# Head of an inducing-point attention and maxout kernel: GpSimd takes the second half of w2−w1, half of w1 comes a second time as fp16, and the first half of hwd is one VectorE copy with two factors

## The chip, the cores and the metric

The kernel runs on one core of one Trainium2 chip. The metric is the device time of one execution in microseconds. Three runs of the kernel before gave 324.2 (median), 323.96 and 324.99.

## What is computed

The reference, cut to what matters (x is 4 × 12544 × 128, inducing 32 × 128, w1 and w2 128 × 1024, w_out 1024 × 128, all fp32):

```python
def mab(q, kv):
    s = scale * (q @ kv.transpose(0, 2, 1))
    s = s - s.max(-1, keepdims=True)
    a = np.exp(s)
    a /= a.sum(-1, keepdims=True) + 1e-09
    return a @ kv
h = mab(I, x)                 # 32 inducing points read the batch
attn = mab(x, h)              # every token reads the 32 results
h1, h2 = attn @ w1, attn @ w2
out = np.maximum(h1, h2) @ w_out
```

The kernel uses max(h1, h2) = h1 + relu(h2 − h1). A token's attention row is a weighted mean of 32 rows of h, so h·(w2−w1), a 32 × 1024 matrix called `hwd`, is made once for each batch, and so is h·(w1·w_out), called `m1`. A token then needs its 32 exponentials e, relu(e·hwd)·w_out + e·m1, and a division by the sum of e.

## The kernel before, in words

**Stages.** The head handles batch 0 alone. It loads x as fp16 (the load casts) in eleven parts, transposes them on TensorE (steps `T`, line 235), copies them from PSUM to SBUF on VectorE or ScalarE (`C`, 246 and 249), scores them against the inducing points (`S`, 258), exponentiates (`X`, 274), and sums h (`H`, 303) and the weights (`E`, 286). After that come the small steps that make `hT`, `hwd` and `m1` of batch 0. The main loop then streams all 392 chunks of 128 tokens of the four batches, and prepares the next batch beside them. All instructions of an engine run in the order in which they are written, so a waiting instruction holds up everything behind it on that engine.

**The head's order** is written out by hand in the string `HEAD` (lines 744 to 750). A letter picks a function, the numbers are its arguments. The last two lines of it, from `h` on, and the two `A` steps and `N0.0` in the lines above, are what this study is about:

- `L` i is `load_x(1, i)` (line 166), a DMA of a part of batch 1, issued by GpSimd. Before all of them GpSimd has issued the loads of batch 0, the four loads of `wf` (line 214: w1 and w2 in fp32, in halves: w1 low, w2 low, w1 high, w2 high) and `woutp` (line 215).
- `A0.2` and `A1.2` are `cast_w1` (774): GpSimd casts the low and the high half of w1 from `wf` to the fp16 tile `w1h`.
- `N0.0` and `N1.0` are `difference` (779): VectorE makes the low and the high half of `w21` = w2 − w1.
- `h` is `small_hT` (451, VectorE), `e` is `small_es` (464, ScalarE), `s` is `small_sums` (490 on TensorE, then 494 and 495 on VectorE): it gives `rs`, the reciprocal of the weight sum, and `rw`, that times 1/scale.
- `D` is `small_hwd0`: a matmul hT × w21 (476) and a copy from PSUM to `hwd` times `rw`, on VectorE (479) or ScalarE (482). `D0.1` makes columns 0 to 255 on ScalarE, `D1.0` columns 256 to 511 on VectorE, `D2.1` columns 512 to 1023 on ScalarE.
- `G0` and `G1` are `score` of blocks 0 and 1 (610, TensorE), `Y` their exponentials (629, ScalarE): `Y0.1` columns 0 to 255 of block 0, `Y0.2` columns 256 to 511, `Y1` all of block 1.
- `W0.1` and `W1.0` are `weights_2`: four transposes of a half of `w1h` (546), copied to `w1T` on ScalarE (552) or VectorE (549). `w` is `weights_3`: w1T × woutp (559), copied to `w1out` on ScalarE (567), from which `small_m1` (518, 526) is made.
- `P0` and `P1` are the first two phases of the main loop.

**A phase** (`phase`, line 1069) is one round of matmuls for four units, one in each quarter of TensorE's rows. Each unit fills a PSUM bank with 512 columns of e·hwd; a relu then empties it on ScalarE (1085) or VectorE (1088). `P0` reads `hwd` columns 0 to 511 and e columns 0 to 255. `P1` reads columns 512 to 1023 of `hwd` in its first quarter. The products relu × woutp (876) follow, an output tile is divided by the sum of e (671 to 681, 907) and stored. Matmuls on a constant tile (833) fill places in which the planner expects TensorE to wait.

**Banks and planner.** Eight PSUM banks serve everything. A model clock in the program (`ck`) decides at build time which bank is taken (the one that the model has free first), which engine gets a relu, and what comes next in the main loop. At the first phase and after the head the model's times are overwritten with fixed numbers; the banks get the times by their rank, so the numbers of the banks may change places while the sequence of the jobs stays.

Of the kernel before, what the change touches and what calls it, by code (L numbers as in the profile page):

```python
# [12 lines left out]
ALU = mybir.AluOpType  # L13
# [89 lines left out]
def kernel(  # L103
# [9 lines left out]
    nc = tc.nc  # L113
    B, N, C = x.shape
    M = inducing.shape[0]
    J = moe_w1.shape[1]
# [3 lines left out]
    scale = 1.0 / math.sqrt(C)  # L120
    P1 = 14
# [17 lines left out]
    ck = Clock()  # L139
    uid = [0]  # L140

    def bank(shape, dtype=F32, only=None):
        i = min(range(8), key=lambda j: ck.bank[j]) if only is None else only
        uid[0] += 1
        return i, psum.tile(shape, dtype, name=f"ps{uid[0]}", tag=f"bank{i}", bufs=1)
# [14 lines left out]
    def load_x(b, i, after=None):  # L160
        k0, n = parts[b][i]
        if after is not None:

            nc.gpsimd.tensor_copy(out=pace, in_=after)  # L164
        for lo, hi in ((0, 65), (65, 128)) if b == 0 and i in (4, 5) else ((0, 128),):
            nc.gpsimd.dma_start(out=xn_at[b, i][lo:hi, 0:n, :], in_=xr[b, lo:hi, k0 : k0 + n, :])  # L166
# [18 lines left out]
    w1h = relup.tile([128, 4096], F16, name="w1h", tag="relu1")[:, 0:J]  # L185
    w21 = consts.tile([C, J], F16, name="w21")
    woutp = consts.tile([128, NJB, C], F16, name="woutp")
    w1T = consts.tile([128, NJB, C], F16, name="w1T")
    w1out = consts.tile([C, C], F16, name="w1out")
# [7 lines left out]
    with tc.manual_schedule(engines={ET.PE, ET.DVE, ET.Activation, ET.Pool, ET.SP}):  # L197
# [14 lines left out]
        for lo in (0, 512):  # L212
            for w, src in enumerate((moe_w1, moe_w2)):
                nc.gpsimd.dma_start(out=wf[:, w, lo : lo + 512], in_=src[:, lo : lo + 512])
        nc.gpsimd.dma_start(out=woutp, in_=moe_w_out.rearrange("(jb j) c -> j jb c", j=128))
        nc.vector.memset(warm, 0.0)
        nc.vector.memset(ones16, 1.0)
# [6 lines left out]
        st = [dict() for _ in range(B)]  # L224
# [242 lines left out]
        def small_hwd0(n, eng=0):  # L467
            if "hwd" not in st[0]:
                st[0]["hwd"] = smp.tile([128, J], F16, name="hwd_0", tag="hwd")
            hwd = st[0]["hwd"]  # L470
            lo, w = ((0, 256), (256, 256), (512, 512), (512, 256), (768, 256))[n]
            bi, ps = bank([128, 512])
            ps = ps[:, 0:w]
            sl = slice(lo, lo + w)
            ck.wait(max(ck.bank[bi], st[0]["hT4r"]), "p1")
            nc.tensor.matmul(out=ps, lhsT=st[0]["hT4"], rhs=w21[:, sl], start=True, stop=True)
            end = ck.run(0.215 * w / 512)
            if eng == 0:
                nc.vector.tensor_scalar(out=hwd[:, sl], in0=ps, scalar1=st[0]["rw"], scalar2=None, op0=ALU.mult)
                ck.bank[bi] = ck.on_dve(end, 0.07 + w / 970.0)  # L480
            else:
                nc.scalar.activation(out=hwd[:, sl], in_=ps, func=AF.Copy, scale=st[0]["rw"])  # L482
                ck.bank[bi] = ck.on_act(end, 0.06 + w / 1200.0)
            st[0]["hwdr"] = max(ck.bank[bi], st[0].get("hwdr", 0.0))

        def small_sums():
            es, ready = st[0]["es"]
            ps = st[0]["eps"]
            ck.wait(ready, "p1")
            nc.tensor.matmul(out=ps[:, 2:3], lhsT=rep32, rhs=es, start=True, stop=True, skip_group_check=True)  # L490
            end = ck.run(0.11)
            st[0]["rs"] = smp.tile([128, 1], F32, name="rs_0", tag="rs_")
            st[0]["rw"] = smp.tile([128, 1], F32, name="rw_0", tag="rw_")
            nc.vector.reciprocal(out=st[0]["rs"], in_=ps[:, 2:3])
            nc.vector.tensor_scalar(out=st[0]["rw"], in0=st[0]["rs"], scalar1=1.0 / scale, scalar2=None, op0=ALU.mult)
            ck.bank[st[0]["eb"]] = st[0]["rsr"] = ck.on_dve(end, 0.34)

        def small_hwd(b):
            st[b]["hwd"] = smp.tile([128, J], F16, name=f"hwd_{b}", tag="hwd")
# [39 lines left out]
        w_of = {}  # L539
# [180 lines left out]
        bi, ps = bank([128, 512])  # L720
        for _ in range(WARM):
            nc.tensor.matmul(out=ps, lhsT=warm[:, 0:128], rhs=warm, start=True, stop=True)
        for n in ("h", "e"):
# [19 lines left out]

        HEAD = """
            T0.0 T0.1 C0.1 I C0.0 L0 T1.0 A0.2 C1.0 T1.1 C1.1 S0 S1 X0 X1 L1 H0 T2.0 E0 T2.1 C2.1 T3.0 C2.0
            A1.2 T3.1 S2 C3.0 X2 T4.0 H1 C3.1 L2 T4.1 S3 T5.0 T5.1 C4.0 H2 X3 C4.1 S4 T6.0 E1 C5.0 H3 T6.1
            X4 C6.0 C6.1 H4 T7.0 C5.1 E2 T7.1 S5 C7.0 T8.1 T8.0 C8.0 C8.1 C7.1 X5 S7 X7 S6 T9.0 H5 C9.0
            T10.0 T10.1 E5 X6 C10.0 C10.1 S8 E6 H7 X8 E4 N0.0 S10 S9 H6 E3 X9 H8 H9 E8 E9 E7 X10 E10 H10 e h
            W0.1 s N1.0 D0.1 G0 Y0.1 G1 Y1 D1.0 D2.1 Y0.2 W1.0 P0 w P1
        """  # L750

        def p1_inducing():
# [192 lines left out]
        def next_job(q):  # L945

            k, u = ptr[q]
            while k < len(blocks) and (q >= len(blocks[k].units) or u >= len(blocks[k].units[q])):
                k, u = k + 1, 0
            ptr[q] = [k, u]  # L950
            if k >= len(blocks):
                return None
            blk = blocks[k]
            if blk.staged is None:
                return None
            if relu_slot(blk, q) is None:
                return None
            return blk, blk.units[q][u]

        def want_linear():  # L960
            while state["lin"] < len(groups) and groups[state["lin"]].full:
                state["lin"] += 1
            if state["lin"] >= len(groups):
                return None
            g = groups[state["lin"]]
            if g.blk.staged is None or finals_left() > LINEAR_AHEAD:
                return None
            if st[g.blk.b].get("m1r", 0.0) > ck.pe + 0.2:
                return None
            return g  # L970
# [25 lines left out]
        def plan_phase(linear=True):  # L996
            jobs = []
            gl = want_linear() if linear else None
            for q in range(4):
                if gl is not None and gl.chunks[0][0] == q:  # L1000
                    jobs.append(("L", q, gl, None))
                    continue
                j = next_job(q)
                if j is not None:
                    jobs.append(("U", q, j[0], j[1]))
            return jobs
# [96 lines left out]
        for b in range(1, B):  # L1103
            base = DONE0[b - 1]
            t_first, t_step = (6, 2.2) if b == 1 else (-6, 3.4)
            for u in range(NU):
                if b == 1:
                    s, turn, acc = 25 + 5 * u, 45 + 1.5 * u, 55 + 2 * u
                else:
                    s = turn = 13 + 8.2 * u  # L1110
# [5 lines left out]
            s, end = int(s), base + int(acc)  # L1116
# [95 lines left out]
        def first_phase(n):  # L1212
            if n == 0:
                ck.pe, ck.act, ck.dve, ck.mode = 18.828, 19.678, 18.404, "col"
                order = sorted(range(8), key=lambda j: ck.bank[j])
                for j, t in zip(order, (17.587, 17.870, 17.927, 18.391, 18.539, 18.728, 19.371, 19.848)):
                    ck.bank[j] = t
                st[0]["hwdr"], st[0]["hT4r"] = 19.371, 17.187
                blocks[0].staged = 18.728
            phase(plan_phase(False))  # L1220

        def score(n):
# [2 lines left out]
        def score_exp(n, part=0):  # L1225
# [2 lines left out]

        steps = {
            "T": p1_transpose, "C": p1_copy, "S": p1_scores, "X": p1_exp, "E": p1_esum, "H": p1_hsum,  # L1230
            "F": fill, "I": p1_inducing, "N": difference, "A": cast_w1, "L": lambda i: load_x(1, i), "h": small_hT, "e": small_es, "s": small_sums,
            "W": weights_2, "G": score, "Y": score_exp, "D": small_hwd0, "P": first_phase, "w": weights_3,
        }
        for step in HEAD.split():
# [4 lines left out]
        order = sorted(range(8), key=lambda j: ck.bank[j])  # L1239
        for j, t in zip(order, (20.325, 20.710, 20.802, 21.002, 21.307, 21.479, 21.904, 21.956)):  # L1240
            ck.bank[j] = t
        st[0]["hwdr"], st[0]["hT4r"], w_of["w1T"] = 19.371, 17.187, 17.870
        blocks[0].staged, blocks[1].staged = 18.728, 19.848
        pending.append((small_m1, (0,)))
        state["stage"] = 2
# [74 lines left out]
```

## Time and profile before

| what | before |
| --- | --- |
| time of three runs | 324.2 us median (323.96 to 324.99) |
| span of the profiled execution, first to last instruction | 322.5 us |
| what lies around the span, by the median | 1.7 us |
| TensorE clock granted, mean | 1.000 |
| the chain that ended last, by engine | PE 93%, DMA 5%, ACT 1% |

The profiled execution's own time is not listed apart from the three runs; its span is 322.5 us, so 1.7 us lie outside by their median. In the rows that follow, PE is TensorE, PEld its weight loads, DVE VectorE, ACT ScalarE, POOL GpSimd and SP SyncE. A row of the timeline gives start and duration in us, the engine, the line of the kernel, the operation with the tiles it writes and reads, and in brackets the idle time before it with what ended it. Neighbouring rows overlap by some hundredths, since a duration runs to the last write; for what an instruction costs in a row of back-to-back ones, take the distance from start to start.

### The profile page before, as it was taken

The page shows a single profiled execution, that of the slowest core. Times are in us where ns is not written, and L with a number is a line of the kernel's source. Part 1 is how long each engine was busy: PE and PEld are TensorE (multiplying, and loading weights), DVE is VectorE, ACT ScalarE, POOL GpSimd, SP SyncE. Part 2 cuts the span into 40 slices and gives each one's busy share as a digit, 9 for nine tenths or more (in the row PEclk, how much of TensorE's full clock was granted, in tenths as well). Part 3 has the DMA queues.
Part 4 walks back from the last instruction along what each step waited for, and adds up shares of the span by engine and source line. Part 5 has one row for each costly group of instructions (what it writes and reads, how often), then busy time and mean ns, then how long its engine had stood idle before and what let it go on. Part 6 is the DMA issues. An engine that isn't in the chain of part 4 may idle for free.

```text
span 322.5 us, 12605 instructions
## 1 busy us (share of the span) xinstructions
PE 315.6 (98%) x5375; PEld 239.8 (74%) x5375; DVE 281.4 (87%) x508; ACT 281.8 (87%) x561; POOL 37.8 (12%) x90
## 2 busy tenths in 40 slices
PE   7899999999999999999999999999999999999996
PEld 3776777777777777777777777777777777777786
DVE  3369999988989998999989989988998999899974
ACT  3779999998978999999898999998869999999960
POOL 7470000000040000000040000000006400302000
PEclk9999999999999999999999999999999999999999
DMA  8999999954279999794279999893424322324233
GB/s 205 207 268 213 218 249 203 210 136 133 100 150 245 221 254 216 181 194 139 99 151 242 218 258 207 160 211 120 118 96 103 135 80 100 109 100 128 87 118 116
DMA packets 77320, 53.99 MB, mean 167 GB/s; under 512 B 56112, under 2 KB 64976, under 8 KB 77264
## 3 DMA queue, kind: packets, MB, share of 16 engines
q1 hardware_dynamic: 71232, 39.42, 50.0%
q0 software_dynamic: 5888, 13.70, 21.7%
q8 instruction: 42, 0.69, 0.9%
q14 instruction: 14, 0.11, 0.1%
q10 hardware_dynamic: 144, 0.07, 0.1%
HBM read 27.28 MB, written 25.69 MB: 164 GB/s over the span
## 4 chain that ended last, share of the span: by engine, by line
PE 93%; DMA 5%; ACT 1%; issue 1%; POOL 0%; DVE 0%; POOLq 0%
PE ps L876 62%; PE ps L1069 22%; DMA xn<-in_x_dram 5%; PE ps L610 2%; PE ps L385 2%; PE ps L329 1%; PE ps L671 1%; PE ps L833 1%; ACT e L629 0%; PE ps L505 0%; ACT hwd L482 0%; PE ps L235 0%; PE ps L303 0%; PE ps L430 0%; PE ps L258 0%
## 5 line engine op out<-in xcount | busy, mean ns | idle before, releaser
L1085 ACT ACTIVATE relu<-ps 128x512 f16<-128x512 f32 x462 | 244.1, 604 | 23.0 <-PE ps L1069 15.0
L1088 DVE TENSOR_SCALAR relu<-ps 128x512 f16<-128x512 f32 x322 | 206.1, 682 | 16.2 <-PE ps L1069 14.8
L876 PE MATMUL ps<-woutp,relu 128*128 128x128 f16 x3136 | 216.9, 220 | 0.0
L876 PEld LDWEIGHTS <-relu 128*128 128x128 f16 x3136 | 176.6, 98 | 39.4 <-issue 28.9
L1069 PE MATMUL ps<-e,hwd 32*128 32x512 f16 (+2 forms) x888 | 88.2, 358 | 0.1
L907 DVE TENSOR_TENSOR o<-ps,rp 128x512 f32<-128x512 f32 (+3 forms) x80 | 51.2, 640 | 1.8 <-PE ps L876 1.3
L1069 PEld LDWEIGHTS <-hwd 32*128 32x128 f16 x888 | 24.5, 91 | 20.9 <-issue 0.8
L1069 PE MATMUL ps<-m,e 32*128 32x128 f16 x381 | 38.7, 217 | 0.0
L1069 PEld LDWEIGHTS <-e 32*128 32x128 f16 x381 | 21.2, 92 | 2.9 <-issue 0.4
L907 DVE TENSOR_TENSOR o<-ps,rpt 128x512 f32<-128x512 f32 (+3 forms) x28 | 17.3, 618 | 4.1 <-PE ps L853 2.2
L166 POOL DMA_DIRECT2D xn<-in_x_dram x33 | 17.8, 553 | 6.7 <-DMA xn<-in_x_dram 4.6
L164 POOL COPY pace<-hacc 128x1 f32<-128x1 f32 x2 | 0.4, 188 | 133.1 <-DVE hacc L418 133.1
L246 DVE COPY xT<-ps 128x768 f16<-128x768 f16 (+6 forms) x11 | 4.8, 458 | 8.9 <-PE ps L235 8.9
L340 ACT ACTIVATE eu<-ps 128x512 f16<-128x512 f32 x18 | 10.9, 614 | 0.1
L629 ACT ACTIVATE e<-ps 128x512 f16<-128x512 f32 (+2 forms) x21 | 10.4, 568 | 0.2 <-PE ps L610 0.2
L235 PE MATMUL ps<-identity,xn 128*128 128x128 f16 x98 | 8.1, 219 | 2.3 <-DMA xn<-in_x_dram 1.8
L535 POOL COPY m1bd<-m 32x128 f16<-32x128 f16 x4 | 1.1, 287 | 76.7 <-DVE m L530 76.6
L249 ACT COPY xT<-ps 128x768 f16<-128x768 f16 (+5 forms) x10 | 6.5, 671 | 3.0 <-PE ps L235 2.9
L698 POOL TENSOR_TENSOR w1T<-den 128x256 f32<-128x256 f16 (+1 forms) x7 | 4.4, 633 | 38.6 <-DMA den<-e 38.6
L700 POOL TENSOR_TENSOR w1T<-w1T 128x64 f32<-128x64 f32 (+4 forms) x28 | 8.4, 302 | 2.2
L235 PEld LDWEIGHTS <-xn 128*128 128x128 f16 x98 | 5.6, 97 | 4.0 <-DMA xn<-in_x_dram 2.2
L610 PE MATMUL ps<-xT,hT 128*32 128x512 f16 (+3 forms) x114 | 8.2, 361 | 0.0
(93 smaller groups left out, 117.0 us busy)
## 6 DMA issues: line engine op xcount, KB each, us to landing
out_dram<-o SPq DMA_DIRECT2D x68, 256.0 KB, 2.8
xn<-in_x_dram POOLq DMA_DIRECT2D x24, 448.0 KB, 10.1
out_dram<-o SPq DMA_DIRECT2D x54, 128.0 KB, 1.8
wf<-in_moe_w_dram POOLq DMA_DIRECT2D x4, 256.0 KB, 5.9
xn<-in_x_dram POOLq DMA_DIRECT2D x3, 224.0 KB, 8.8
xT<-xn SPq DMA_TRANSPOSE x42, 3.8
xf<-in_x_dram SPq DMA_DIRECT2D x1, 512.0 KB, 3.7
xf<-in_x_dram SPq DMA_DIRECT2D x1, 384.0 KB, 4.2
```

What stands on the lines that cost most here:

```text
L166: nc.gpsimd.dma_start(out=xn_at[b, i][lo:hi, 0:n, :], in_=xr[b, lo:hi, k0 : k0 + n, :])
L235: nc.tensor.transpose(ps[:, j, :], xn_at[0, i][:, g + j, :], identity16)
L249: nc.scalar.copy(out=dst, in_=ps[:, 0:m, :])
L340: nc.scalar.activation(out=eu, in_=ps, func=AF.Exp, scale=scale, accum_out=st[b]["es"][:, u : u + 1])
L610: nc.tensor.matmul(out=ps[32 * q : 32 * (q + 1), 128 * t : 128 * (t + n)], lhsT=hq, rhs=xT[:, c : c + n, :], start=True, stop=True, tile_p ...
L629: nc.scalar.activation(out=blk.e2[:, lo:hi], in_=ps[:, lo:hi], func=AF.Exp, scale=st[0]["rs"] if blk.b == 0 else scale,)
L700: nc.gpsimd.tensor_add(acc[:, :, 0:n], acc[:, :, 0:n], acc[:, :, n : 2 * n])
L876: nc.tensor.matmul(out=g.ps[:, 128 * c : 128 * (c + 1)], lhsT=g.blk.relu[q][:, 128 * (jb * w4 + t) : 128 * (jb * w4 + t + 1)], rhs=woutp[: ...
L907: nc.vector.tensor_mul(osb[:, 0:n, :], g.ps[:, 0 : n * C].rearrange("p (s c) -> p s c", s=n), rp)
L1069: nc.tensor.matmul(**seq[i])
L1085: nc.scalar.activation(out=dst, in_=src, func=AF.Relu)
L1088: nc.vector.tensor_scalar(out=dst, in0=src, scalar1=0.0, scalar2=None, op0=ALU.max)
```

## The change

The w1 high half is loaded a second time, cast to fp16 by the DMA, and GpSimd's cast of it (`A1.2`) is gone. GpSimd does the high half of `w21` (`N1.1` for `N1.0`), ahead of the load `L2`. `D0` is now one copy of 512 columns on VectorE, which multiplies by `rs` and by 1/scale, and so needs no `rw`; `D1` is the other 512 columns, on ScalarE, with `rw`, which has a step of its own (`r`) behind `D0.0`. `Y1` stands behind `P0`, `W1.0` ahead of `D1.1`, and `Y0.2` right behind `D1.1`. The model clock gets fixed numbers ahead of `P1` too.

```diff
             for w, src in enumerate((moe_w1, moe_w2)):
                 nc.gpsimd.dma_start(out=wf[:, w, lo : lo + 512], in_=src[:, lo : lo + 512])
+        nc.gpsimd.dma_start(out=w1h[:, 512:J], in_=moe_w1[:, 512:J])
         nc.gpsimd.dma_start(out=woutp, in_=moe_w_out.rearrange("(jb j) c -> j jb c", j=128))
...
-            lo, w = ((0, 256), (256, 256), (512, 512), (512, 256), (768, 256))[n]
+            lo, w = ((0, 512), (512, 512))[n]
...
             if eng == 0:
-                nc.vector.tensor_scalar(out=hwd[:, sl], in0=ps, scalar1=st[0]["rw"], scalar2=None, op0=ALU.mult)
+                nc.vector.tensor_scalar(
+                    out=hwd[:, sl], in0=ps, scalar1=st[0]["rs"], scalar2=1.0 / scale, op0=ALU.mult, op1=ALU.mult
+                )
...
             nc.vector.reciprocal(out=st[0]["rs"], in_=ps[:, 2:3])
+            ck.bank[st[0]["eb"]] = st[0]["rsr"] = ck.on_dve(end, 0.2)
+
+        def small_rw():
             nc.vector.tensor_scalar(out=st[0]["rw"], in0=st[0]["rs"], scalar1=1.0 / scale, scalar2=None, op0=ALU.mult)
-            ck.bank[st[0]["eb"]] = st[0]["rsr"] = ck.on_dve(end, 0.34)
+            ck.on_dve(0.0, 0.14)
...
-            A1.2 T3.1 S2 C3.0 X2 T4.0 H1 C3.1 L2 T4.1 S3 T5.0 T5.1 C4.0 H2 X3 C4.1 S4 T6.0 E1 C5.0 H3 T6.1
+            T3.1 S2 C3.0 X2 T4.0 H1 C3.1 N1.1 L2 T4.1 S3 T5.0 T5.1 C4.0 H2 X3 C4.1 S4 T6.0 E1 C5.0 H3 T6.1
...
-            W0.1 s N1.0 D0.1 G0 Y0.1 G1 Y1 D1.0 D2.1 Y0.2 W1.0 P0 w P1
+            W0.1 s D0.0 r G0 Y0.1 G1 W1.0 D1.1 Y0.2 P0 Y1 w P1
...
                 st[0]["hwdr"], st[0]["hT4r"] = 19.371, 17.187
                 blocks[0].staged = 18.728
+            else:
+                ck.pe, ck.act, ck.dve = 19.709, 20.832, 20.575
+                order = sorted(range(8), key=lambda j: ck.bank[j])
+                for j, t in zip(order, (18.728, 19.371, 19.848, 20.113, 20.325, 20.710, 20.802, 21.002)):
+                    ck.bank[j] = t
...
-        st[0]["hwdr"], st[0]["hT4r"], w_of["w1T"] = 19.371, 17.187, 17.870
+        st[0]["hwdr"], st[0]["hT4r"], w_of["w1T"], w_of["w1out"] = 19.371, 17.187, 17.870, 21.002
```

More of the change, by code (lines that the diff above doesn't have):

```diff
@@ L1230 @@
             "T": p1_transpose, "C": p1_copy, "S": p1_scores, "X": p1_exp, "E": p1_esum, "H": p1_hsum,
-            "F": fill, "I": p1_inducing, "N": difference, "A": cast_w1, "L": lambda i: load_x(1, i), "h": small_hT, "e": small_es, "s": small_sums,
+            "F": fill, "I": p1_inducing, "N": difference, "A": cast_w1, "L": lambda i: load_x(1, i), "h": small_hT, "e": small_es, "s": small_sums, "r": small_rw,
             "W": weights_2, "G": score, "Y": score_exp, "D": small_hwd0, "P": first_phase, "w": weights_3,
```

## The prediction, made before the changed kernel was run

> **What bounds the kernel now.** First the page: busy shares and the chain that ended last.
>
> ```profile
> span 322.5 us, 12605 instructions
> PE 315.6 (98%) x5375; PEld 239.8 (74%) x5375; DVE 281.4 (87%) x508; ACT 281.8 (87%) x561; POOL 37.8 (12%) x90
> PE 93%; DMA 5%; ACT 1%; issue 1%; POOL 0%; DVE 0%; POOLq 0%
> ```
>
> TensorE is the bound, and the 5% and the 1% of DMA and ScalarE in the chain lie where the kernel starts. The stages tell where that ends.
>
> ```profile
> 22.00:23.00 1.00, 0.83 (x10) 0.39 (x6) 0.95 (x2) 0.98 (x3) 1.00 (x3) 1.00 1.35 225
> 23.00:24.00 1.00, 1.00 (x22) 0.71 (x19) 0.76 (x2) 1.00 (x3) 1.00 (x2) 1.00 1.07 215
> 24.00:25.00 1.00, 0.82 (x17) 0.44 (x15) 1.00 (x3) 1.00 (x4) 0.05 (x1) 1.00 1.11 224
> ...
> 29.00:40.00 11.00, 11.00 (x186) 8.37 (x184) 10.47 (x20) 10.20 (x20) 0.00 (x0) 1.00 1.10 214
> ```
>
> The columns after the length are PE, PEld, DVE, ACT and POOL busy. From 22 to 25 us TensorE has gaps in two of three stretches (0.83, 0.82), and ScalarE has none (0.98, 1.00, 1.00). From 29 us on TensorE has none. So whatever the change does to the moment at which the main loop gets under way is carried, one for one, to the end: nothing behind 29 us can take it up, and nothing there is edited. (That the later order is the same I take from the diff: 20.832 is the model's time of ScalarE at `P0`, 19.678, with two relus at 0.477 and the 0.2 that it books for `w`, and 21.002 is that plus 0.17. The fixed numbers put back the state that the program had without them; only bank numbers change places.)
>
> The chain in order of time says what sets the start:
>
> ```profile
> 22.02 0.47 ACT hwd L482
> ...
> 24.38 0.50 ACT relu L1085
> ...
> 24.92 0.24 PE ps L671 x4
> ```
>
> From 22.02 the chain is ScalarE alone: the first quarter of hwd, `Y0.1` and `Y1`, the high half of hwd, `Y0.2` (their rows stand below), then the first relu until 24.88, and only then TensorE again. The change takes the first of them away and puts `Y1` last. That is the gain on offer. The question is whether ScalarE then has its next input in time.
>
> **Part by part: GpSimd.** Its queue in order, and what the loads took to land:
>
> ```profile
> 15.82 0.54 POOL L214 DMA_DIRECT2D wf<-in_moe_w_dram x1 [0.47 <-DMA xn<-in_x_dram]
> 16.96 0.90 POOL L215 DMA_DIRECT2D woutp<-in_moe_w_out_dram x1 [0.61 <-DMA xn<-in_x_dram]
> 17.85 0.54 POOL L222 MEMSET m1bd<- 128x512 f16 x1
> 18.32 0.57 POOL L166 DMA_DIRECT2D xn<-in_x_dram x1
> 19.63 0.61 POOL L774 CAST w1h<-wf 128x512 f16<-128x512 f32 x1 [0.74 <-DMA wf<-in_moe_w_dram]
> 20.19 0.53 POOL L166 DMA_DIRECT2D xn<-in_x_dram x1
> 20.85 0.62 POOL L774 CAST w1h<-wf 128x512 f16<-128x512 f32 x1
> ...
> 10.04 7.70 DMA xn<-in_x_dram
> ...
> wf<-in_moe_w_dram POOLq DMA_DIRECT2D x1, 256.0 KB, 5.6
> ...
> woutp<-in_moe_w_out_dram POOLq DMA_DIRECT2D x1, 256.0 KB, 6.0
> ```
>
> The issue of a load can wait for an earlier x load to land (the brackets). The new load takes woutp's place at 16.96 and 0.54 to issue. woutp then waits, I take it, for the next x load, the one issued at 10.04 that landed 7.70 later, at 17.74: it issues from 17.80 to 18.70, 0.84 later than now. The memset and `L0` follow, 18.70 + 0.47 + 0.57 = 19.74. The cast `A0.2` now sits 0.74 idle for its data until 19.63, so it moves only by 0.11. `L1` comes 0.56 behind it and the next step 0.66 behind `L1`: GpSimd is free for `N1.1` at 20.96.
>
> There it must wait, which VectorE did not have to: the high half of w2 is the last wf load, issued at 15.82 and landed 5.6 later, 21.42; 0.05 for the semaphore (the lag of TensorE behind VectorE, below) makes 21.47. Behind `N1.1` on GpSimd are only `L2` to `L6`. Who reads them are SP's transposes of batch 1, and the waits of SP name no x load, so the delay of these loads by about 1 us costs nothing. SP's queue itself is not edited.
>
> The rows for the price of the subtraction, from the groups with their shapes kept apart:
>
> ```profile
> L698 POOL TENSOR_TENSOR w1T<-den 128x256 f32<-128x256 f16 x6 | 4.0, 667 | 38.6 <-DMA den<-e 38.6
> L700 POOL TENSOR_TENSOR w1T<-w1T 128x128 f32<-128x128 f32 x6 | 2.7, 456 | 0.5
> L700 POOL TENSOR_TENSOR w1T<-w1T 128x64 f32<-128x64 f32 x7 | 2.2, 321 | 0.5
> ...
> L698 POOL TENSOR_TENSOR w1T<-den 128x128 f32<-128x128 f16 x1 | 0.4, 427 | 0.0
> ```
>
> No row shows a 128x512 subtraction on GpSimd. From below it costs the cast of the same size, 0.62; from above the fp32 rows of line 700 carried on, (456 − 321)/64 = 2.1 ns an element, 456 + 384 × 2.1 = 1.27. Line 698 gives (667 − 427)/128 = 1.88, so 667 + 256 × 1.88 = 1.15. It is the nearest in size with two inputs, and I take it. So `N1.1` ends at 21.47 + 1.15 = 22.62 (bounds 22.09 to 22.74).
>
> The Trainium skill, GPSIMD Engine Reference, section 4.1 Engine selection, speaks against this move: it sends elementwise operations with two inputs to VectorE, and calls GpSimd about twice as slow. By that rule twice VectorE's 0.69 for the same subtraction (next fence) would be an estimated 1.38, and the sum below 0.23 us more. The add rows of this trace (1.88 ns an element) bear out the direction; no row here shows the size itself.
>
> **Part by part: TensorE, VectorE, ScalarE.** The rows of now:
>
> ```profile
> 21.86 0.69 DVE L779 TENSOR_TENSOR w<-wf 128x512 f16<-128x512 f32 x1
> 21.77 0.15 DVE L495 TENSOR_SCALAR rw<-rs 128x1 f32<-128x1 f32 x1
> 23.64 0.69 DVE L1088 TENSOR_SCALAR relu<-ps 128x512 f16<-128x512 f32 x1
> ...
> 22.14 0.28 PE L476 MATMUL ps<-w,hT 128*128 128x256 f16 x1
> 22.60 0.38 PE L476 MATMUL ps<-w,hT 128*128 128x512 f16 x1 [0.17 <-DVE w L779]
> 22.81 0.39 PE L546 MATMUL ps<-identity,w1h 128*128 128x128 f16 x4
> 23.13 0.40 PE L1069 MATMUL ps<-e,hwd 32*128 32x128 f16 x10
> 23.49 0.62 PE L559 MATMUL ps<-woutp,w1T 128*128 128x128 f16 x8
> 24.43 0.39 PE L1069 MATMUL ps<-e,hwd 32*128 32x256 f16 x8
> ...
> 22.40 0.47 ACT L629 ACTIVATE e<-ps,rs 128x256 f16<-128x256 f32 x1
> 22.75 0.69 ACT L629 ACTIVATE e<-ps,rs 128x512 f16<-128x512 f32 x1
> 23.32 0.70 ACT L482 ACTIVATE hwd<-ps,rw 128x512 f16<-128x512 f32 x1
> 23.89 0.49 ACT L629 ACTIVATE e<-ps,rs 128x256 f16<-128x256 f32 x1
> 24.25 0.62 ACT L1085 ACTIVATE relu<-ps 128x512 f16<-128x512 f32 x1
> 25.20 0.31 ACT L567 CAST w1out<-ps 128x128 f16<-128x128 f32 x1
> 25.35 0.66 ACT L1085 ACTIVATE relu<-ps 128x512 f16<-128x512 f32 x1
> ```
>
> *VectorE* loses `N1.0` (0.69) and trades a copy of 256 columns for one of 512. No row shows the copy with two factors; the nearest is the relu of that shape, 0.69, and I take that (two factors at double would be 1.4, nothing a saving). It starts when `rw` starts now, 21.77, and ends at 22.46, ahead of all that waits for it; `rw` behind it costs 0.15, and is done before `D1.1`.
>
> *The new load* queues behind the last wf load. The first wf load let the cast start at 19.63 and the fourth landed at 21.42, so they are (21.42 − 19.63)/3 = 0.60 apart, and the new one, of as many bytes read, lands at 22.02; at worst it lands where woutp does now, 16.96 + 6.0 = 22.96. `W1.0` comes behind `G1` on TensorE, where 22.14 now shows the next matmul, and 0.06 for the wider `D0` on top: 22.2. It hardly waits. woutp, now there at 22.96, lands 0.60 later, at 23.56, so `w`, now at 23.49, waits for it about 0.1; the wait of `P1` below covers that.
>
> *TensorE* then reaches `D1.1` at about 22.4 and waits for `N1.1`: 22.62 + 0.05 (22.60 now is 0.05 behind VectorE's end, 22.55) = 22.67. `P0`, `w` and `P1` queue behind it. `P0` follows by the 0.21 that lie now between 22.60 and 22.81: 22.88, against 23.13. Good, but the start does not hang on it.
>
> *ScalarE* does `Y0.1` from about 22.05, where the first quarter of hwd starts now (22.02), to 22.40 (22.75 − 22.40 = 0.35). Its next is the high half of hwd, one matmul (0.38) and 0.05 behind 22.67: 23.10. Now `Y1` fills that place; after the change ScalarE is idle for 0.7. From start to start the rows cost 0.57 (hwd), 0.36 (`Y0.2`), 0.95 (two relus, 24.25 to 25.20), 0.57 (`Y1`) and 0.15 (w1out). So `Y0.2` starts at 23.67, the first relu of `P0` at 24.03 (ends 0.62 later, 24.65, against 24.87), `Y1` at 24.98, w1out at 25.55, and the first relu of `P1` at 25.70, against 25.35. One operation of 0.38 is saved, and 0.7 of idle put in its place.
>
> *P1*. By rank its four banks are now those of the high hwd, of `W1.0`, of block 0's scores and of the first relu of `P0` on VectorE; its last matmuls start at 24.43, behind `Y0.2` (23.89 + 0.49 = 24.38). In the changed order of the model's times (`G1` and `w` last) they are those of the high hwd, of block 0's scores, and of the first relus of `P0` on VectorE and on ScalarE. The last of these ends at 24.65: 24.70 with the semaphore, 0.27 later than 24.43. VectorE's relus of `P1` and the first products behind them move by as much, and the next phase, which needs banks of ScalarE's relus of `P1` (0.35 later), by 0.27 to 0.35.
>
> **Sum**, on the profiled span: 322.5 + 0.3 = 322.8; with the 1.7 us around it, by the median of the runs, 324.2 + 0.3 = **324.5 us**. By bounds: with `N1.1` at 0.62 `D1.1` comes right behind `W1.0`, 22.2 + 0.21 = 22.41, 0.26 sooner, and the sum is about 0; at 1.27 it is +0.4.
>
> **Rivals.**
> (1) *The saved work shows.* VectorE and ScalarE are both busy without a gap around 24 us, and the change takes the 0.38 of the first quarter (22.02 to 22.40) off ScalarE. It is faster if `D1.1` starts before 22.40, and has all of the 0.38, 323.8, if `D1.1` starts at 22.0, so that ScalarE goes on from `Y0.1` without a gap. For it: the wait of TensorE for VectorE's subtraction (0.17 in the row at 22.60) and the wider gap of ScalarE are both settled by one load, and loads shift by some tenths. Against it: the load at 21.42 with GpSimd's least, 0.62, is 22.09, and `W1.0` stands ahead.
> (2) *A load is late.* If the new one lands at 22.96 instead of 22.02, `W1.0` starts at 23.01, `D1.1` at 23.22, 0.55 behind my 22.67: 324.2 + 0.3 + 0.55 = 325.05. For it speaks that DMA engines are full in this stage (share above 1.0 in each row); against, that the wf loads come 0.60 apart, so that the queue and not a fixed delay sets their landing.
> (3) *The sizes are right, but the main loop differs*: the swapped banks meet a relu that is late somewhere, or TensorE's places for the constant matmuls take the shift up. Either sign, up to 1 us. Against it: no gap of TensorE from 29 us on.
> (4) *Nothing changes*: hidden by other waits, 324.2 ± 0.1; that is my lower bound of `N1.1`.
>
> **Chances.** Forecast (324.2 to 324.8) 0.50; rival 1 (323.2 to 324.1) 0.15; rival 2 (324.8 to 325.6) 0.15; rival 3 0.10, halved; rival 4 0.10. A measurement of this kernel tells about 0.3% from no change, 0.97 us: faster means below 323.23, slower above 325.17. Of rival 1 a fifth and of rival 3 half lies below: 0.08. Of rival 2 half, of rival 3 half, and 0.05 for a forecast that is right in kind and too small: 0.18. The rest, 0.74, is no change by that bound. The range takes in rival 1's middle and most of rival 2: 323.6 to 325.5.
>
> **What would show each step.** In the profile after: the subtraction on POOL (line of `difference`) starts at 21.5 behind a wait for wf and lasts about 1.15; ScalarE has a gap of some 0.7 us between `Y0.1` and the high half of hwd; the last matmuls of `P1` start at 24.7; w1out is cast at 25.55. Wrong if the gap is under 0.35 (then rival 1), if `W1.0` and not `D1.1` is what TensorE waits for (rival 2), or if TensorE shows idle time behind 29 us that it does not show now (rival 3).

## The result, and the profile after

| | before | after |
| --- | --- | --- |
| median of 21 runs each | 324.15 us | 324.71 us |
| lowest to highest | 323.96 to 325.06 | 324.65 to 325.32 |
| ratio, 95% interval | | 1.0016 (1.0010 to 1.0022) |
| span of the profiled execution | 322.5 us | 322.9 us |

The changed kernel is 0.56 us slower by the medians, and the interval leaves out 1. By the prediction's bound of 0.3% this is no change; by the runs it is a small loss. The page and the stages of the changed kernel answer to the first fences of the prediction (columns after the length: PE, PEld, DVE, ACT, POOL busy).

```profile
span 322.9 us, 12605 instructions
PE 91%; DMA 4%; POOL 2%; issue 1%; ACT 0%; DVE 0%; POOLq 0%
```

```profile
22.00:23.00 1.00, 0.61 (x9) 0.28 (x5) 0.85 (x3) 0.39 (x1) 1.00 (x2) 1.00 1.63 192
...
24.00:25.00 1.00, 0.75 (x12) 0.40 (x10) 0.91 (x2) 1.00 (x3) 1.00 (x3) 1.00 1.05 214
...
29.00:40.00 11.00, 11.00 (x185) 8.37 (x185) 10.47 (x20) 10.20 (x21) 0.00 (x0) 1.00 1.13 219
```

POOL, GpSimd, is new in the chain, with 2%; most of that is the issuing of x loads before 7 us, and the subtraction alone, 1.28 us, is 0.4%. ScalarE, which had been busy for 0.98 of the stretch from 22 to 23 us, is busy for 0.39 of it, and TensorE for 0.61 instead of 0.83. From 29 us on the two profiles are alike. The loss lies between 21 and 26 us. The chain of the changed kernel, in order of time, shows its path:

```profile
15.69 5.65 DMA wf<-in_moe_w_dram
21.33 0.02 issue
21.36 0.02 POOLq L785
21.37 0.10 issue
21.48 1.28 POOL w L785
22.76 0.04 issue
22.80 0.39 PE ps L477
23.19 0.02 issue
23.21 0.69 ACT hwd L485
23.90 0.36 ACT e L635
24.27 0.50 ACT relu L1091
24.76 0.04 issue
24.81 0.43 PE ps L1075 x3
25.24 0.02 issue
25.26 0.70 DVE relu L1094
```

Read it link by link. The last load of w2 lands at 21.33. GpSimd subtracts for 1.28. TensorE's matmul for the high half of hwd (`D1.1`) starts at 22.80. ScalarE copies it from 23.21, does `Y0.2`, and its first relu ends at 24.76. That frees the last bank that `P1` waits for, at 24.81, where it was 24.43 before, and VectorE's next relu waits for `P1` until 25.26. Each link is one that the prediction named.

The rows of the timeline show the gaps in brackets, here for ScalarE and TensorE:

```profile
21.92 0.47 ACT L635 ACTIVATE e<-ps,rs 128x256 f16<-128x256 f32 x1 [0.31 <-PE ps L616]
23.21 0.69 ACT L485 ACTIVATE hwd<-ps,rw 128x512 f16<-128x512 f32 x1 [0.82 <-PE ps L477]
...
25.68 0.29 ACT L573 CAST w1out<-ps 128x128 f16<-128x128 f32 x1
...
22.80 0.38 PE L477 MATMUL ps<-w,hT 128*128 128x512 f16 x1 [0.39 <-POOL w L785]
24.81 0.37 PE L1075 MATMUL ps<-e,hwd 32*128 32x256 f16 x7 [0.17 <-ACT relu L1091]
...
319.79 0.22 PE L859 MATMUL ps<-m1bd,e 128*128 128x128 f16 x1
```

ScalarE waits 0.82 for `D1.1`, and that waits 0.39 for GpSimd. w1out is cast 0.48 later than before (25.20). The very last matmul starts at 319.79, in the kernel before at 319.43: 0.36 later, near the 0.38 of `P1`, carried through nearly 300 us. The heads of the two profiles are not level, though. The rows of `hT` and of the last matmul, first of the kernel before, then `hT` of the changed one:

```profile
21.03 0.29 DVE L451 TENSOR_SCALAR hT<-ps 128x128 f16<-128x128 f32 x1
319.43 0.22 PE L853 MATMUL ps<-m1bd,e 128*128 128x128 f16 x1
...
20.82 0.28 DVE L452 TENSOR_SCALAR hT<-ps 128x128 f16<-128x128 f32 x1
```

`hT` starts 0.21 sooner in the profile after. From `hT` to the last matmul it is 298.40 us before and 298.97 after, 0.57 longer. A sooner `hT` does not help the changed kernel, since `D1.1` goes by the load of w2.

### The profile page after: what moved, and what is told of

It reads as the page before. It is cut to its first block, busy times and chain, and to the rows that moved or that the text cites. A ratio compares the mean times of both kernels' runs of the same rounds, so it can differ in the third digit from the quotient of the medians.

```text
span 322.9 us, 12605 instructions
## 1 busy us (share of the span) xinstructions
PE 315.7 (98%) x5374; PEld 239.7 (74%) x5374; DVE 281.0 (87%) x507; ACT 281.3 (87%) x560; POOL 39.4 (12%) x91
## 4 chain that ended last, share of the span: by engine, by line
PE 91%; DMA 4%; POOL 2%; issue 1%; ACT 0%; DVE 0%; POOLq 0%
PE ps L882 62%; PE ps L1075 23%; DMA xn<-in_x_dram 3%; PE ps L616 2%; DMA wf<-in_moe_w_dram 2%; PE ps L386 2%; PE ps L330 1%; POOL xn L166 1%; PE ps L677 1%; PE ps L839 0%; PE ps L511 0%; POOL w L785 0%; PE ps L431 0%; DVE relu L1094 0%; ACT hwd L485 0%
```

## The experiments

Theory A: `D1.1` waits for GpSimd's subtraction, ScalarE stands idle meanwhile, since `Y1` no longer fills the place, and the start of the main loop moves. Rival B: the second load of w1 costs the time. Rival C: `P1`'s swapped banks cost it. In each experiment the sequence of the main loop's jobs is that of the kernel before.

**1. Undo the move to GpSimd alone** (of the changed kernel):

```diff
-            T3.1 ... C3.1 N1.1 L2 ...
+            T3.1 ... C3.1 L2 ...
-            W0.1 s D0.0 r G0 Y0.1 G1 W1.0 D1.1 Y0.2 P0 Y1 w P1
+            W0.1 s r N1.0 D0.0 G0 Y0.1 G1 W1.0 D1.1 Y0.2 P0 Y1 w P1
```

> The changed kernel with the subtraction of the high half back on VectorE, ahead of the low hwd copy, and rw ahead of both; everything else of the change stays, the second load too. Theory A (the changed kernel is slower because TensorE's matmul for the high half of hwd waits for GpSimd's subtraction, 22.80, and ScalarE idles 0.9 us for it): that matmul starts behind W1.0 at about 22.42, the high hwd on ScalarE at 22.85 instead of 23.21, P1's last matmuls at 24.45 instead of 24.81; 0.36 faster than the changed kernel, 324.35, 1.0006 of the kernel before. Theory B (the second load costs the time): as the changed kernel, 1.0016. Theory C (P1's swapped banks cost it, by the wait for ScalarE's first relu): nearly as the changed kernel or a part of A's gain.

Measured: 324.42 us, 1.0001 of the kernel before (0.9993 to 1.0010). The rows of its timeline:

```profile
22.45 0.38 PE L477 MATMUL ps<-w,hT 128*128 128x512 f16 x1
...
22.86 0.69 ACT L485 ACTIVATE hwd<-ps,rw 128x512 f16<-128x512 f32 x1 [0.35 <-PE ps L477]
...
23.11 0.40 PE L1075 MATMUL ps<-e,hwd 32*128 32x128 f16 x10 [0.29 <-DVE hwd L480]
```

`D1.1` starts at 22.45 without a wait, and ScalarE's gap is 0.35 instead of 0.82. The second load is still there and the order is the changed one, so B as the whole cause falls. The program also gives `P1` the same four banks as in the changed kernel, so C as the whole cause falls too: these banks cost nothing where `D1.1` is not late. A new wait of 0.29 shows: `P0` now waits for VectorE's copy of the low hwd, which stands behind the subtraction.

**2. Put only `Y1` back** ahead of the high hwd, and leave the subtraction on GpSimd:

```diff
-            W0.1 s D0.0 r G0 Y0.1 G1 W1.0 D1.1 Y0.2 P0 Y1 w P1
+            W0.1 s D0.0 r G0 Y0.1 G1 Y1 W1.0 D1.1 Y0.2 P0 w P1
```

> The changed kernel with Y1 back between Y0.1 and the high hwd on ScalarE. GpSimd's subtraction and the second load stay. Theory A with its second half (it is the idle place on ScalarE that costs, not the wait of TensorE as such): Y1 fills the 0.9 us; the high hwd still starts at 23.21, but w1out is cast at 25.1 instead of 25.68 and P1 waits no longer for a relu on ScalarE, 24.3 instead of 24.8; about 324.05, 0.9997 of the kernel before (0.9990 to 1.0003). Theory A in its plain form (the late matmul alone sets the time) and theory B: as the changed kernel, 1.0016.

Measured: 324.42 us, 1.0001 (0.9993 to 1.0010); 0.9997 was expected, with a range up to 1.0003.

```profile
23.05 0.38 PE L477 MATMUL ps<-w,hT 128*128 128x512 f16 x1 [0.49 <-POOL w L785]
...
24.43 0.56 PE L1075 MATMUL ps<-e,hwd 32*128 32x128 f16 x10
...
23.46 0.69 ACT L485 ACTIVATE hwd<-ps,rw 128x512 f16<-128x512 f32 x1 [0.38 <-PE ps L477]
24.51 0.49 ACT relu L1091
25.36 0.28 ACT L573 CAST w1out<-ps 128x128 f16<-128x128 f32 x1
...
319.62 0.22 PE L859 MATMUL ps<-m1bd,e 128*128 128x128 f16 x1
```

Here the last w2 load came later and `D1.1` started at 23.05, 0.25 later than in the changed kernel's profile. The last matmul nevertheless starts 0.17 sooner (319.62 against 319.79). The profile of the same kernel in run 4 has `D1.1` almost where the changed kernel has it (22.80), and its last matmul starts 0.39 sooner:

```profile
22.83 0.38 PE L477 MATMUL ps<-w,hT 128*128 128x512 f16 x1 [0.23 <-POOL w L785]
...
319.40 0.22 PE L859 MATMUL ps<-m1bd,e 128*128 128x128 f16 x1
```

So the late matmul alone is not the loss; what stands behind it counts. The gain does not lie in ScalarE's first relu, which ends at 25.00 here (the chain's row of 24.51) against 24.76 in the changed kernel: the high hwd ahead of it still goes by `D1.1`. Two other things differ. `P1` no longer waits for that relu: its ten matmuls (row of 24.43) run through without a wait, and VectorE's four relus follow each other without a gap, where in the changed kernel the third waits 0.35 for `P1`. And w1out, with `Y1` no longer ahead of it, is cast at 25.36 instead of 25.68. The first comes from the banks: by the order of the model's times, `Y1`'s late read of its scores keeps a bank taken in the changed kernel, and `P1` takes one behind ScalarE's relu instead. So the part of C that is left is this bank together with a late `D1.1`. How much of the gain is the bank and how much the order on ScalarE stays open, since this edit changes both.

**3. The second load alone**, in the kernel before, in place of `A1.2`:

```diff
+        nc.gpsimd.dma_start(out=w1h[:, 512:J], in_=moe_w1[:, 512:J])
-            A1.2 T3.1 S2 ...
+            T3.1 S2 ...
```

> The kernel before with only the second load of w1 in place of GpSimd's cast of the high half; subtraction, copies and order as before. Theory A: no wait that counts, 324.15, 1.000 (0.9995 to 1.0005); woutp lands at 23.4, just ahead of its use at 23.49. Theory B: the whole loss, 1.0016.

Measured: 324.32 us, 1.0001 (0.9992 to 1.0010). B falls. But the load is not free of traces:

```profile
23.77 0.62 PE L560 MATMUL ps<-woutp,w1T 128*128 128x128 f16 x8 [0.36 <-DMA woutp<-in_moe_w_out_dram]
```

`w` waits 0.36 for woutp, behind the new load in the queue. The time shows no loss: in the kernel before the last matmuls of `P1` wait for `Y0.2` until 24.43, and here all ten run from 24.32 on.

**4. The changed kernel without the load** (GpSimd casts, then subtracts), beside the changed kernel itself and runs 1 and 2 once more, all on one chip:

```diff
-        nc.gpsimd.dma_start(out=w1h[:, 512:J], in_=moe_w1[:, 512:J])
-            T3.1 S2 ...
+            A1.2 T3.1 S2 ...
```

> The changed kernel itself, on one chip with the three that follow, so that they can be set against each other. 324.7, 1.0013 to 1.0016 of the kernel before.

> The changed kernel without the second load: GpSimd casts the high half of w1, then subtracts. Theory A (GpSimd's subtraction and ScalarE's gap): the subtraction waits for the last wf load anyway and starts at 21.5 as before; as the changed kernel, 1.0013 to 1.0016. Theory B (the load costs): back at 1.0000.

> The changed kernel with the subtraction back on VectorE, once more, beside the changed kernel on the same chip. Theory A: 0.3 to 0.5 us below it, 1.0000 to 1.0006 of the kernel before.

> The changed kernel with only Y1 back ahead of the high hwd, once more, beside the changed kernel on the same chip. Theory A with its second half: 0.2 to 0.4 us below the changed kernel, though TensorE still waits for GpSimd's subtraction.

| kernel | median us | ratio to before (95% interval) |
| --- | --- | --- |
| changed | 324.70 | 1.0014 (1.0004 to 1.0025) |
| changed, without the load | 324.67 | 1.0014 (1.0005 to 1.0023) |
| changed, subtraction on VectorE | 324.37 | 1.0003 (0.9994 to 1.0012) |
| changed, `Y1` ahead of the high hwd | 324.36 | 1.0006 (0.9997 to 1.0015) |

Without the load the subtraction starts at 21.38, with it at 21.43 in the profile of the repeat, since it waits for the last wf load in both:

```profile
21.38 1.27 POOL L784 TENSOR_TENSOR w<-wf 128x512 f16<-128x512 f32 x1
```

The load neither costs nor gains time here, but it comes close to it. In the profile of the repeat `w` waits for woutp, which stands behind the new load in the queue, and the chain runs over that wait and not over the subtraction:

```profile
23.98 0.62 PE L565 MATMUL ps<-woutp,w1T 128*128 128x128 f16 x8 [0.53 <-DMA woutp<-in_moe_w_out_dram]
```

The last matmul starts at 319.75 there, and at 319.69 without the load, so the two waits end nearly together.

Each of the two undoings takes 0.33 or 0.34 off the changed kernel on this chip; by the medians of the first runs, which were not taken beside each other, it is 0.29. With the subtraction on VectorE ten of eleven runs lie below the lowest of the changed kernel (324.56), with `Y1` put back six of eleven. The intervals to the kernel before overlap each other; this comparison and the next two runs are what the verdict rests on.

**5. More of the suspected wait**: GpSimd's subtraction done a second time, once by half (`N5.1`, 256 columns) and once in full.

```diff
-            ... C3.1 N1.1 L2 ...
+            ... C3.1 N1.1 N5.1 L2 ...      (by half)
+            ... C3.1 N1.1 N1.1 L2 ...      (in full)
```

> The changed kernel with half of GpSimd's subtraction done a second time (0.66 us more). If a longer wait costs in proportion: 324.71 + 0.66 = 325.4, 1.0037 of the kernel before, with the granted clock at 1.0. If the fall of the granted clock that the doubled subtraction showed (0.56 to 0.50 from 26.2 to 29.6 us) comes with this gap of TensorE too: 326.5 to 327, 1.008.

Measured: 325.46 us, 1.0037 (1.0024 to 1.0051). The half took 0.73 on GpSimd; `D1.1` starts 0.83 later than in the changed kernel, and so does the last matmul:

```profile
23.63 0.38 PE L477 MATMUL ps<-w,hT 128*128 128x512 f16 x1 [1.06 <-POOL w L785]
...
320.62 0.22 PE L859 MATMUL ps<-m1bd,e 128*128 128x128 f16 x1
```

320.62 − 319.79 = 0.83. The wait is passed on one for one, as A says; by B and C nothing would change.

> The changed kernel with GpSimd's subtraction of the high half done twice in a row, the second with the same result. It doubles the suspected wait. Theory A: the high hwd's matmul at 24.07 instead of 22.80 and all behind it 1.27 later: 324.71 + 1.27 = 326.0, 1.0057 of the kernel before. Theories B and C: no change against the changed kernel, 1.0016.

Measured: 327.5 us, 1.0099 (1.0085 to 1.0114): 2.8 more than the changed kernel, where 1.27 was expected. `D1.1` starts at 24.20, 1.40 later than in the changed kernel's profile, so the wait itself accounts for half. The stages show a second cost; the column before the last two is the granted TensorE clock:

```profile
22.40:24.20 1.80, 0.14 (x4) 0.02 (x1) 0.53 (x3) 0.12 (x1) 1.72 (x3) 1.00 1.32 210
24.20:26.20 2.00, 1.73 (x22) 0.91 (x22) 1.18 (x2) 1.59 (x4) 2.00 (x4) 1.00 1.07 214
26.20:26.40 0.20, 0.20 (x7) 0.19 (x6) 0.11 (x1) 0.20 (x1) 0.20 (x2) 0.56 1.07 215
26.40:29.40 3.00, 3.00 (x32) 1.72 (x27) 2.06 (x6) 2.18 (x6) 0.39 (x1) 0.50 1.07 210
29.40:29.80 0.40, 0.40 (x5) 0.28 (x3) 0.40 (x1) 0.40 (x2) 0.00 (x0) 0.70 1.05 206
```

From 26.2 to 29.6 us TensorE runs at half its clock. In the profile the last matmul starts at 322.22, 2.43 later than in the changed kernel: 1.40 of wait and 1.03 more. The profiled execution and one other of the four took 327.09 and 327.28 us at a mean clock of 0.995; the other two took 327.72 and 328.2 at 0.99. No other profile here shows a lower clock between 17 and 300 us.

**6. The move alone**, in the kernel before:

```diff
-            ... C3.1 L2 ...
+            ... C3.1 N1.1 L2 ...
-            W0.1 s N1.0 D0.1 ...
+            W0.1 s D0.1 ...
```

> The kernel before with only the subtraction of the high half moved to GpSimd, behind its cast of w1. If the move costs by itself (theory A in its plain form): D2.1 on TensorE at 22.82 instead of 22.60, and the loss of the changed kernel in full, 1.0016. If it is the move together with the empty place on ScalarE (theory A with its second half): Y1 still fills ScalarE until 23.3, the high hwd starts when it does now, P0 and VectorE's first relu come 0.2 later, and 0.1 to 0.2 us are lost, 1.0003 to 1.0006.

Measured: 324.55 us, 1.0008 (0.9999 to 1.0017), between the two branches and nearer to the second.

```profile
22.91 0.38 PE L476 MATMUL ps<-w,hT 128*128 128x512 f16 x1 [0.59 <-POOL w L779]
...
23.32 0.69 ACT L482 ACTIVATE hwd<-ps,rw 128x512 f16<-128x512 f32 x1
...
23.95 2.49 DVE L1088 TENSOR_SCALAR relu<-ps 128x512 f16<-128x512 f32 x4
```

TensorE waits 0.59, longer than in the changed kernel (`W1.0` does not stand ahead of this matmul here), and ScalarE does not wait at all: its high hwd starts at 23.32 as before. What is late is `P0` and with it VectorE's first relu, 23.95 against 23.64. This is the kernel before with its own banks, so the move seems to have a price of its own, 0.28 us by the medians, about half of the loss. The interval takes in 1, so this share is not shown; that the order and the banks of the changed kernel make the rest is argued from runs 2 and 4.

**7. Two versions meant to beat both**, without the load, with `Y1` ahead of the high hwd:

```diff
-            W0.1 s D0.0 r G0 Y0.1 G1 W1.0 D1.1 Y0.2 P0 Y1 w P1
+            W0.1 s r N1.0 D0.0 G0 Y0.1 G1 Y1 W1.0 D1.1 Y0.2 P0 w P1      (all on VectorE)
+            W0.1 s N4.0 D0.0 r G0 Y0.1 G1 Y1 W1.0 D1.1 Y0.2 P0 w P1      (split: N4.0 here, N5.1 on GpSimd ahead of L2)
```

> A version meant to beat both: no second load (GpSimd casts as in the kernel before), subtraction on VectorE behind rw and ahead of the low hwd, the one copy of 512 columns with two factors, Y1 between Y0.1 and the high hwd. By theory A ScalarE has no gap: one operation of 0.38 less, w1out cast at 24.85 to 24.9 instead of 25.2; P1 is then held by VectorE's first relu at 24.3 instead of 24.4. 0.1 to 0.3 us faster than the kernel before, 0.9995 (0.9990 to 1.0002). If ScalarE's gap is not what counts: 1.0000 or slower, since VectorE gives the low hwd later (23.0).

Measured: 324.30 us, 1.0000 (0.9991 to 1.0009). ScalarE has no gap, but the gain does not come:

```profile
22.51 0.74 DVE L479 TENSOR_SCALAR hwd<-ps,rs 128x512 f16<-128x512 f32 x1
...
23.31 0.40 PE L1074 MATMUL ps<-e,hwd 32*128 32x128 f16 x10 [0.29 <-DVE hwd L479]
```

The low hwd ends at 23.25 behind the subtraction on VectorE, `P0` waits for it until 23.31, and the 0.38 saved on ScalarE meets a VectorE that is late.

> As the version without the second load, but with the subtraction split: 256 columns on VectorE ahead of the low hwd, 256 on GpSimd at the same time. If a VectorE operation with two SBUF inputs and a GpSimd operation run side by side: the VectorE part lasts 0.42, the low hwd is there at 22.6, P0 at 22.7, P1 at 24.0; 0.3 to 0.4 faster than the kernel before, 0.9989. If the one that starts second waits for the other (the 0.87 of VectorE's first subtraction beside GpSimd's cast in the runs so far, against 0.69 in the kernel before): the VectorE part ends at 22.5, the low hwd at 23.15, and it is 0.9995 to 1.0003.

Measured: 324.53 us, 1.0005 (0.9996 to 1.0013). The second branch is the one that came, somewhat worse than foreseen (1.0003 at most):

```profile
21.70 0.73 POOL L784 TENSOR_TENSOR w<-wf 128x256 f16<-128x256 f32 x1 [0.31 <-DMA wf<-in_moe_w_dram]
...
21.72 0.99 DVE L784 TENSOR_TENSOR w<-wf 128x256 f16<-128x256 f32 x1
```

The two halves start 0.02 apart, and VectorE's 256 columns take 0.99, longer than its 512 alone (0.69). They end at 22.71, 0.28 behind the end of GpSimd's half (22.43), so VectorE spent most of the time waiting. This version is not a clean test of the split: `r` stands behind `D0.0`, so the high hwd on ScalarE also waits for `rw`, by 0.44. Neither version beats the kernel before.

## Why the prediction was right

The direction, the mechanism and the place were right; the time was 0.2 us higher than the forecast of 324.5, within its range. Point by point:

| step | foreseen | measured |
| --- | --- | --- |
| last w2 load lands | 21.42 | 21.33 |
| subtraction starts | 21.47 | 21.48 |
| subtraction lasts | 1.15 (0.62 to 1.27) | 1.28 |
| `D1.1` starts | 22.67 | 22.80 |
| ScalarE's gap | 0.7 | 0.82 |
| `P0` on TensorE | 22.88 | 23.11 |
| high hwd on ScalarE | 23.10 | 23.21 |
| last matmuls of `P1` | 24.70 | 24.81 |
| w1out cast | 25.55 | 25.68 |
| sum on the span | +0.3 | +0.4 |

- **The mis-sized term is the subtraction**, 1.15 against 1.28. Of two rows the one nearer in size was taken, with fp16 input; the fp32 rows, carried on, gave 1.27, the bound, and were the right ones. What follows on ScalarE and in `P1` is late by the same 0.11 to 0.13, and the sum by that bound, +0.4, is what the spans show. The Trainium skill's rule of about twice VectorE's time (GPSIMD Engine Reference, section 4.1 Engine selection) gave an estimated 1.38; the trace has 1.28, which is 1.28/0.69 = 1.9 times.
- **Luck in the start of the subtraction.** The load landed 0.09 sooner than foreseen, and GpSimd's instruction came 0.15 behind the landing (the chain's rows from 21.33 to 21.48) and not 0.05, a lag that the prediction had taken from TensorE behind VectorE. The two errors cancel; from profile to profile the start of the subtraction moves between 21.38 and 21.73.
- **`P0` was read wrong**, without effect on the sum: it comes 0.31 behind `D1.1`, not 0.21, which was the distance to another step. So it starts when it did before (23.11 against 23.13) and not 0.25 sooner.
- **The rest, from 0.4 on the spans to 0.56 by the medians**, has no step of its own. The changed kernel's profiled execution took 324.66 with a span of 322.9, so 1.76 lie around it; with as much around the span of before, that execution took 324.26, which is 0.11 above its median. So most of the difference may be that the profile of before was not of its median run. The uneven heads point to the whole of it: from `hT` on the changed kernel is 0.57 longer, and its repeat 0.46 (298.86), by the medians 0.56 and 0.50. The two ways of counting overlap, and neither is shown by more than these profiles.
- **"From 29 us on nothing can take it up"** was right: 0.36 at the last matmul, and 0.83 for 0.83 with the half subtraction.
- **The second load and woutp**: `w` was said to wait 0.1 for woutp. In the profile it does not (23.47 against 23.49 before); in run 3 it waits 0.36, in the profile of the repeat 0.53. The cover named, the wait of `P1`, was needed there.
- **The rivals.** (1), that the saved work shows, did not come, also where ScalarE had no gap (run 7): VectorE's low hwd was next in line. (2), a late load, did not decide the time (runs 3 and 4), though woutp behind the new load came onto the chain in the repeat. (3) and (4) did not come.
- **The banks**: that `P1`'s last matmuls wait for ScalarE's first relu is in the row of 24.81. It was read from the order of the model's times. Run 1 has the same banks and no loss, so the banks cost only together with the late `D1.1`; how the loss splits between this bank and the order on ScalarE was not measured.

## What to carry to other kernels

Taking an operation off a busy engine gains only if the next input of that engine is there when the operation is gone; look for the producer that becomes last, and here it was a load that landed at 21.3 us plus the slower engine to which the work had been moved. An order that looks late for one operation (`Y1` ahead of the high hwd) may be what fills a wait, so move a filler only together with a proof that the wait is gone, and look which buffers the move hands to the next steps. Price an operation on an engine that has never run it by the rows with its input type, not only by those of its size.

## What the runs showed of the hardware that was not expected

**After a gap of 1.7 us TensorE ran at half its clock for a while.** With the subtraction done twice, TensorE was nearly idle from 22.5 to 24.2 us, and its granted clock fell to 0.50 two microseconds after it had gone back to work, for 3.4 us (26.2 to 29.6). With the gap of 1.06 us of the half subtraction the clock stayed at 1.00 in the profile. So in these two profiles a `D1.1` that is 0.83 us later costs 0.83, and one that is 1.40 later costs 2.43. That the gap set off the fall is argued from them; what length of gap does it was not measured. The Trainium skill, TensorE: Matmul & The Clock Gate, section What's actually happening, describes a clock that is set by free-running windows of activity of about 3.4 us, and lets it fall after an idle window. The 3.4 us at half clock agree with the length of such a window; the gap of 1.7 us, about half of one, does not agree with a whole idle window as the condition.

**VectorE with two inputs from SBUF waits for GpSimd.** Beside the split, it shows in a step that the change did not mean to touch. The low subtraction of the changed kernel, on VectorE, and GpSimd's cast:

```profile
19.69 0.65 POOL L780 CAST w1h<-wf 128x512 f16<-128x512 f32 x1
...
20.04 0.85 DVE L785 TENSOR_TENSOR w<-wf 128x512 f16<-128x512 f32 x1 [0.67 <-DMA wf<-in_moe_w_dram]
```

VectorE's subtraction takes 0.85 where it took 0.69 in the kernel before, because it starts at 20.04, before the cast ends at 20.34; it ends 0.55 after the cast's end. The Trainium skill, SBUF — State Buffer, section Who interferes with whom, has the rule: a VectorE instruction with two SBUF inputs and a GpSimd instruction that reads SBUF exclude each other. The rows agree with it in direction: in the nine profiles in which this subtraction starts before the cast ends it takes 0.85 to 0.87, in the five in which it starts later 0.69. They do not show a full wait, since the cast ran on for 0.30 and only 0.16 was added. It cost next to nothing here: `hT` starts at 20.82, just behind the last sum of h, and `D1.1` waits for GpSimd anyway.
